# Attention with beacons and an MoE layer on one core: the first loads, a fourth buffer of probabilities, two of raw Q/K

## The chip, the cores and the metric

The kernel runs on one core of a Trainium2 chip. The metric is the device time of one execution in microseconds (us). Before the change the median of five runs is 351.29 us (350.4 to 353.74). Another execution was profiled; durations and waits come from that one.

## What is computed

For each of 8 batches and 8 heads there are 576 queries, keys and values of 64 elements, and 16 "beacon" keys and values in front of them. Every query sees all beacons, and the keys up to its own place. The heads' results are set side by side to a row of 512 elements per token (4608 tokens), and two matrix products follow with a leaky ReLU between them.

```python
scores = scale * np.matmul(q, k_all.transpose(0, 1, 3, 2))   # k_all: 16 beacons, then k
scores = np.where(causal, -1000000000.0, scores)
a = np.exp(scores - scores.max(-1, keepdims=True))
a /= a.sum(-1, keepdims=True) + 1e-09
attn = np.matmul(a, v_all)
x = attn.transpose(0, 2, 1, 3).reshape(B * S, H * D)
h = x @ w_in                    # 512 -> 2048
out = np.maximum(0.01 * h, h) @ w_out   # 2048 -> 512
```

## The kernel before, in words

**Head pairs.** The unit of attention is a pair of heads: 4 pairs to a batch, 32 in all, counted by `g`; `divmod(g, 4)` gives the batch and the place in it. Keys lie on the 128 partitions in five chunks (`ROWS`, `OFF`; the first has the 16 beacons and 112 keys). For a pair, `score(g, n)` (L295) makes four groups of transposed scores, n = 0 to 3, in PSUM: 2 x 512, 2 x 464, 2 x 416 and 2 x 288 columns, with causal parts that would be all zero left out. ScalarE takes each group's exponential out of PSUM (L315) into the pair's buffer of probabilities, `aT`. There are two PSUM buffers for scores (`ps_sc`), three of `aT` (`a_bufs`, L97) and three of the transposed keys `kT` (L98). The triangle on the diagonal is then set to zero: by VectorE with a stored triangle for pairs 0 and 1 (`masks_by_tri`, L335), by GpSimd with four affine selects for all others (`masks`, L346).

**Values.** `value(g, half)` (L368) multiplies the probabilities with `v_aug`, the values with a column of ones, in two halves of the queries: the first half needs chunks 0 to 2 of the values, the second all five. VectorE divides by the sums (L395, L396) into `x_nat`. `finish(g)` transposes `x_nat` on TensorE and VectorE copies it to `xT` (L413), from which the MoE part reads. Four PSUM buffers (`ps_one`) serve values, transposes and MoE groups alike.

**MoE.** Tokens go in 9 chunks of 512. `moe1` (L416) makes one group of 128 hidden units for a chunk: four matmuls and a leaky ReLU by ScalarE (L429); a chunk has 16 of them. `moe2` (L434) does a quarter of 128 tokens' output, also four matmuls. `fill()` (L464) issues the next group of either kind that is allowed. A chunk of tokens can start when the pairs that it needs are finished; the first one needs pair 3. Groups 0 to 7 of a chunk read the first half of `w_in`, groups 8 to 15 the second.

**Loads.** Queries and keys are loaded by GpSimd's queue, which casts float32 to bfloat16 on the way (`load_qk`, L120 and L133): a call for one batch and two pairs (`grp`), with `es` telling which of the two pairs. Tiles `q_raw` and `k_raw` come from `qkpool`, three buffers of each. Values are loaded in float32 on SyncE's queue (`load_v`, L209 to L218) in six DMAs, the first of which waits for the DMA that `after` names; `cast_v` casts them chunk by chunk, on GpSimd. Weights are loaded and cast by GpSimd's queue in halves (L110, L114). For batches 0 and 1, TensorE transposes queries and keys (`t_q`, L235, 18 small transposes each) and VectorE copies them out; from batch 2 on, GpSimd brings them into order (`permute`, L160), a transposing DMA on SyncE's queue turns them (`turn_pairs`, L266), and GpSimd copies them to their place (`in_order`, L279).

**The very first pair.** `load_first_pair` (L141) loads the queries of pair 0 in float32 on SyncE's queue and its keys in float32 on ScalarE's queue, behind the beacon keys of batches 0 and 1. VectorE casts the queries (L510), ScalarE and VectorE a half of the keys each (L511, L512). Ahead of them, `keep_busy(n)` (L477) lets TensorE do n products of the identity with itself, whose result nobody reads.

**Order.** The order on every engine is the order in which the program issues instructions (`manual_schedule`, L488)[...]. The last part of the program is therefore the schedule: a prologue, then a loop over `g` in which pairs 0 to 7 have orders written out by hand, and pairs from 8 on share one order in which MoE groups fill slots between scores and values. `loads(g)` and `loads_after(g)` put loads, casts and the DMA transposes into GpSimd's and SyncE's order.

Of the kernel before, what the change touches and what calls it, by code (L numbers as in the profile page):

```python
# [9 lines left out]
BF16 = mybir.dt.bfloat16  # L10
# [5 lines left out]
def kernel(  # L16
# [11 lines left out]
    nc = tc.nc  # L28

    B, H, S, D = q.shape  # L30
# [10 lines left out]
    RI = 9  # L41
    RP = S // RI
# [25 lines left out]

    singles = ctx.enter_context(tc.tile_pool(name="singles", bufs=1))
    rawpool = ctx.enter_context(tc.tile_pool(name="rawpool", bufs=2))  # L70
    qkpool = ctx.enter_context(tc.tile_pool(name="qkpool", bufs=3))
    natpool = ctx.enter_context(tc.tile_pool(name="natpool", bufs=2))
    turnpool = ctx.enter_context(tc.tile_pool(name="turnpool", bufs=2))
    headpool = ctx.enter_context(tc.tile_pool(name="headpool", bufs=2))
# [19 lines left out]
        for t in v_bufs:  # L94
            nc.gpsimd.memset(t[:, :, :, D : D + 1], 1.0)

    a_bufs = [singles.tile([128, 2, ACOLS], BF16, name=f"aT{i}") for i in range(3)]  # L97
    k_bufs = [singles.tile([128, NKB * 128], BF16, name=f"kT{i}") for i in range(3)]  # L98

    def make_pads():  # L100
# [16 lines left out]

    qk_raw = {}

    def load_qk(b, grp, es=(0, 1)):  # L120


        if (b, grp) not in qk_raw:
            qk_raw[b, grp] = (
                qkpool.tile([128, 2, RI, D], BF16, name="q_raw"),
                qkpool.tile([128, 2, RI, D], BF16, name="k_raw"),
            )
        for e in es:
            if b == 0 and grp == 0 and e == 0:
                continue  # L130
            h0 = 4 * grp + 2 * e
            for src, dst in zip((q, k), qk_raw[b, grp]):
                dma = nc.gpsimd.dma_start(  # L133
                    out=dst[e * RP : (e + 1) * RP],
                    in_=src[b, h0 : h0 + 2].rearrange("h (p i) d -> p h i d", i=RI),
                )
        return dma

    first_raw = []

    def load_first_pair():  # L141
        load_beacon_k(0, 2, nc.scalar)
        t = rawpool.tile([128, NKB, H, D], FP32, name="v_raw")
        flat = t[0:RP].rearrange("p c h d -> p (c h d)")
        n = 2 * RI * D
        for i in range(2):
            first_raw.append(flat[:, i * n : (i + 1) * n].rearrange("p (h i d) -> p h i d", h=2, i=RI))
        for eng, src, dst in zip((nc.sync, nc.scalar), (q, k), first_raw):
            last = eng.dma_start(out=dst, in_=src[0, 0:2].rearrange("h (p i) d -> p h i d", i=RI))
        return last  # L150


    first_cast = [
        natpool.tile([128, RI, 2, D], BF16, name=n)[0:RP].rearrange("p i e d -> p (i e d)").rearrange(
            "p (h i d) -> p h i d", h=2, i=RI
        )
        for n in ("q_nat", "k_nat")
    ]

    def permute(b, grp, which):  # L160

# [73 lines left out]
    def t_q(g, which, copy=nc.vector.tensor_copy):  # L235
# [10 lines left out]
            dst = kT[:, NB : NB + S]  # L246
        ps = ps_one.tile([128, 1024], BF16, name="tp", tag="one")
        raw = qk_raw[b, grp][which]
        if g == 0:
            raw = first_cast[which]  # L250
        for i in range(RI):
            for h in range(2):
                nc.tensor.transpose(
# [41 lines left out]
    def score(g, n):  # L295
        qT, kT = qk[g]
        if n == 0:
            probs[g] = a_bufs[g % 3]
        aT = probs[g]
        parts = SCORES[n]  # L300
        sc = ps_sc.tile([128, 2, 512], FP32, name="sc", tag="sc")
        c0 = parts[0][3]
        for c, q0, w, col in parts:
            for par in range(2):
                ps_ = slice(par * 64, par * 64 + 64)
                nc.tensor.matmul(  # L306
                    out=sc[:, par, col - c0 : col - c0 + w],
                    lhsT=kT[ps_, c * 128 : (c + 1) * 128],
                    rhs=qT[ps_, q0 : q0 + w],
                    start=True,  # L310
                    stop=True,
                    skip_group_check=True,
                )
        w = sum(p[2] for p in parts)
        nc.scalar.activation(  # L315
            out=aT[:, :, c0 : c0 + w], in_=sc[:, :, 0:w], func=AF.Exp, scale=0.125
        )
# [178 lines left out]
        }  # L496
    )
    with order:
        first = load_first_pair()
        make_identity(nc, ident)  # L500
        load_qk(0, 0)
        load_qk(0, 1)
        load_v(0, after=first)
        make_pads()
        cast_beacon_k(0, 2, nc.scalar.copy)
        keep_busy(24)
        beacon_transposes(0, 2)
        beacon_columns(0, nc.vector)
        beacon_columns(1, nc.vector)
        nc.vector.tensor_copy(out=first_cast[0], in_=first_raw[0])  # L510
        nc.scalar.copy(out=first_cast[1][:, 0], in_=first_raw[1][:, 0])  # L511
        nc.vector.tensor_copy(out=first_cast[1][:, 1], in_=first_raw[1][:, 1])  # L512
        keep_busy(18)
        t_q(0, 0)
        keep_busy(4)
        t_q(0, 1, nc.scalar.copy)
        keep_busy(3)
        make_tri()
        make_ones()
        beacon_columns(2, nc.gpsimd)  # L520
        cast_v(0, nc.gpsimd, 0, 1)
        load_qk(1, 0, (0,))

        def loads(g):
            b, hp = divmod(g, NPAIR)
            if g == 1:
                beacon_columns(3, nc.gpsimd)
                cast_v(0, nc.gpsimd, 1, 3)
                load_v(1, after=load_qk(1, 0, (1,)))
                cast_v(0, nc.gpsimd, 3, 5)  # L530
                load_w_in(0)
            elif g == 2:
                beacon_columns(4, nc.gpsimd)
            elif g == 3:
# [38 lines left out]
        for g in range(NG + 3):  # L573
            if has(g):
                loads(g)

            if g < 5:

                score(g, 0)
                score(g, 1)  # L580
                t_q(g + 1, 0)
                t_q(g + 1, 1)
                if g in (1, 2):
                    masks_by_tri(g - 1)
                if g >= 3:
                    value(g - 2, 0)
                if g < 2:
                    keep_busy(3)
                score(g, 2)
# [3 lines left out]
                if g < 2:  # L593
                    keep_busy(4)
                if g == 2:
                    value(g - 2, 0)
                if g >= 2:
                    value(g - 2, 1)
                if g >= 3:
                    finish(g - 3)  # L600
                if g > 1:
                    masks(g)
                if g == 4:
                    value(3, 0)
                continue

            if g == 5:

                score(5, 0)
                value(3, 1)  # L610
                score(5, 1)
                finish(2)
                score(5, 2)
                finish(3)
                fill()
                score(5, 3)
                masks(5)
                fill()
                t_q(6, 0)
                t_q(6, 1)  # L620
                fill()
                fill()
                continue

            if g == 6:
# [14 lines left out]
                load_beacon_k(2, B, nc.gpsimd)  # L640
                fill()
                fill()
                value(4, 0)
                value(4, 1)
                continue

            if g == 7:
                score(7, 0)
                score(7, 1)
                value(5, 0)  # L650
                finish(4)
                value(5, 1)
                score(7, 2)
                score(7, 3)
                load_qk(2, 0)
                masks(7)
                finish(5)
                value(6, 0)
                fill()
                value(6, 1)  # L660
                fill()
                fill()
                finish(6)
                value(7, 0)
                fill()
                value(7, 1)
                fill()
# [4 lines left out]
            if g == 8:  # L672
# [8 lines left out]
                while done1[0] + done2[0] < 22:  # L681
                    fill()
                beacon_transposes(2, B)
                while done1[0] + done2[0] < 30:
                    fill()
                in_order(8)
                in_order(9)
# [75 lines left out]
```

## Time and profile before

| | before |
|---|---|
| median of five runs | 351.29 us |
| the profiled execution | 351.35 us |
| its span, first to last instruction | 349.5 us |
| TensorE busy (share of the span) | 339.3 us (97%) |
| ScalarE busy | 187.4 us (54%) |
| GpSimd busy | 196.5 us (56%) |
| VectorE busy | 98.0 us (28%) |
| moved by DMA | 40.88 MB, 117 GB/s on average |

The profile names engines PE (TensorE; PEld is its weight load), DVE (VectorE), ACT (ScalarE), POOL (GpSimd) and SP (SyncE); a q behind a name is an engine's DMA-issuing side. In a timeline, a row has its start and its duration in us, then engine, line, operation and "result<-sources", and in brackets how long the engine had been idle before it and what released it; rows of one kind in a row are merged (x12). In the chain of waits, a row has a start and a duration in us, and then what the end of the program was waiting for at that time. In a table by stretches, a row has the stretch, its length, the busy time and number of instructions of each engine, the granted clock of TensorE, the mean busy share of the DMA engines, and the GB/s that they moved.

### The profile page before, as it was taken

How to read it: one execution, taken by the hardware profiler on the slowest of the kernel's cores; microseconds unless marked ns; L12 is line 12 of the kernel's file. 1: busy time of each engine (PE TensorE's matmuls, PEld its weight loads, DVE VectorE, ACT ScalarE, POOL GpSimd, SP SyncE). 2: the span in 40 equal slices, each digit the busy share in tenths (PEclk: the TensorE clock that was granted, in tenths of full speed). 3: DMA queues.
4: the chain of work that ended last, by engine and by line, in shares of the span. 5: the costliest groups of instructions: out<-in, count | busy, mean ns of one | idle time of the engine just before them, and what ended most of it. 6: DMA issues, size and time to landing. Idle time of an engine off the chain costs nothing.

```text
span 349.5 us, 7405 instructions
## 1 busy us (share of the span) xinstructions
PE 339.3 (97%) x3045; PEld 171.7 (49%) x3045; DVE 98.0 (28%) x240; ACT 187.4 (54%) x277; POOL 196.5 (56%) x335
## 2 busy tenths in 40 slices
PE   7889999899999999999999999999999999999996
PEld 6565554334554444444544444455444554444444
DVE  3794530123342222322321223222321331000121
ACT  4978756565456863486347833784368304633300
POOL 7596926688899799777976779667321100000000
PEclk9999999999999999999999999999999999999999
DMA  8999999968988894992489419980110011000012
GB/s 164 198 159 200 181 213 158 191 120 160 227 167 122 158 164 96 187 197 54 79 181 184 93 33 192 183 125 31 49 45 0 2 73 49 0 30 32 30 60 92
DMA packets 85121, 40.88 MB, mean 117 GB/s; under 512 B 69040, under 2 KB 79280, under 8 KB 85088
## 3 DMA queue, kind: packets, MB, share of 16 engines
q1 hardware_dynamic: 72544, 26.52, 36.4%
q0 software_dynamic: 12128, 13.54, 25.1%
q10 hardware_dynamic: 416, 0.36, 0.5%
q8 instruction: 24, 0.39, 0.5%
q14 instruction: 9, 0.07, 0.1%
HBM read 37.22 MB, written 9.44 MB: 134 GB/s over the span
## 4 chain that ended last, share of the span: by engine, by line
PE 79%; DMA 12%; POOL 3%; DVE 2%; SPq 2%; issue 1%; ACT 0%; POOLq 0%
PE acc L444 36%; PE acc L422 28%; PE av L386 7%; PE sc L306 6%; DMA v_raw<-in_v_dram 5%; DMA bk_raw<-in_beacon_k_dram 4%; DMA q_turn<-q_nat 1%; PE tp L408 1%; DMA v_raw<-in_k_dram 1%; DVE osb L453 1%; SPq L218 1%; POOL v_aug L227 1%; DVE xT L413 1%; POOL w_out_sb L114 0%; POOL aT L355 0%
## 5 line engine op out<-in xcount | busy, mean ns | idle before, releaser
L422 PE MATMUL acc<-xT,w_in_sb 128*128 128x512 bf16 x576 | 139.3, 379 | 1.6 <-DVE xT L413 1.4
L315 ACT ACTIVATE aT<-sc 128x1024 bf16<-128x1024 f32 (+3 forms) x128 | 103.7, 869 | 66.7 <-PE sc L306 66.7
L444 PE MATMUL acc<-w_out_sb,gT 128*128 128x512 bf16 (+1 forms) x592 | 139.0, 374 | 0.0
L429 ACT ACTIVATE gT<-acc 128x512 bf16<-128x512 f32 x144 | 85.8, 601 | 74.2 <-PE acc L422 73.9
L444 PEld LDWEIGHTS <-gT 128*128 128x128 bf16 x592 | 53.2, 98 | 58.4 <-issue 6.1
L422 PEld LDWEIGHTS <-w_in_sb 128*128 128x128 bf16 x576 | 51.8, 98 | 59.6 <-issue 4.6
L453 DVE COPY osb<-acc 128x512 f32<-128x512 f32 (+1 forms) x37 | 25.1, 677 | 128.8 <-PE acc L444 128.0
L355 POOL TENSOR_SCALAR_AFFINE_SELECT aT<-aT 128x224 bf16<-128x224 bf16 (+1 forms) x120 | 48.7, 450 | 18.6 <-PE av L386 9.9
L286 POOL COPY qT<-q_turn 128x576 bf16<-128x576 bf16 x24 | 28.6, 1191 | 40.2 <-PE sc L306 21.2
L386 PEld LDWEIGHTS <-aT 128*128 128x128 bf16 (+1 forms) x960 | 36.9, 98 | 15.5 <-issue 2.4
L386 PE MATMUL av<-v_aug,aT 128*128 128x65 bf16 (+1 forms) x960 | 40.0, 194 | 0.7 <-POOL v_aug L227 0.7
L306 PE MATMUL sc<-qT,kT 64*128 64x80 bf16 (+4 forms) x384 | 35.8, 283 | 3.0 <-ACT aT L315 1.5
L396 DVE TENSOR_TENSOR x_nat<-av,rec 128x384 bf16<-128x384 f32 x64 | 31.4, 491 | 2.2
L286 POOL COPY kT<-k_turn 128x576 bf16<-128x576 bf16 x24 | 28.6, 1190 | 0.8 <-DMA k_turn<-k_nat 0.6
L413 DVE COPY xT<-tp 128x576 bf16<-128x576 bf16 x32 | 14.5, 453 | 45.2 <-PE tp L408 45.2
L395 DVE RECIPROCAL rec<-av 128x6 f32<-128x6 f32 x64 | 11.9, 186 | 52.8 <-PE av L386 52.8
L306 PEld LDWEIGHTS <-kT 64*128 64x128 bf16 x384 | 12.3, 94 | 28.5 <-issue 16.2
L227 POOL CAST v_aug<-v_raw 128x512 bf16<-128x512 f32 (+1 forms) x35 | 20.6, 632 | 5.9 <-DMA v_raw<-in_v_dram 5.9
L133 POOL DMA_DIRECT2D q_raw<-in_q_dram x31 | 19.6, 632 | 5.1 <-DMA w_out_sb<-in_moe_w_out_dram 4.9
L133 POOL DMA_DIRECT2D k_raw<-in_k_dram x31 | 19.7, 634 | 3.8 <-DMA w_out_sb<-in_moe_w_out_dram 2.8
L408 PEld LDWEIGHTS <-x_nat 128*128 128x128 bf16 (+2 forms) x160 | 11.1, 97 | 6.7 <-DVE rec L395 0.2
L167 POOL COPY q_nat<-q_raw 128x1152 bf16<-128x1152 bf16 x12 | 13.9, 1160 | 0.4 <-DMA q_raw<-in_q_dram 0.4
(43 smaller groups left out, 92.3 us busy)
## 6 DMA issues: line engine op xcount, KB each, us to landing
out_dram<-osb SPq DMA_DIRECT2D x35, 256.0 KB, 2.4
v_raw<-in_v_dram SPq DMA_DIRECT2D x24, 256.0 KB, 5.1
q_raw<-in_q_dram POOLq DMA_DIRECT2D x31, 144.0 KB, 5.6
k_raw<-in_k_dram POOLq DMA_DIRECT2D x31, 144.0 KB, 5.8
w_in_sb<-in_moe_w_in_dram POOLq DMA_DIRECT2D x2, 1024.0 KB, 9.4
w_out_sb<-in_moe_w_out_dram POOLq DMA_DIRECT2D x2, 1024.0 KB, 13.2
v_raw<-in_v_dram SPq DMA_DIRECT2D x8, 224.0 KB, 4.0
v_raw<-in_v_dram SPq DMA_DIRECT2D x8, 160.0 KB, 4.5
```

What stands on the lines that cost most here:

```text
L133: dma = nc.gpsimd.dma_start(out=dst[e * RP : (e + 1) * RP], in_=src[b, h0 : h0 + 2].rearrange("h (p i) d -> p h i d", i=RI),)
L227: eng.tensor_copy(out=dst[0 : ROWS[c], c, :, 0:D], in_=t[0 : ROWS[c], c])
L286: nc.gpsimd.tensor_copy(out=dst.rearrange("c (p i) -> c p i", i=RI), in_=t[:, :, e].rearrange("c i p -> c p i"),)
L306: nc.tensor.matmul(out=sc[:, par, col - c0 : col - c0 + w], lhsT=kT[ps_, c * 128 : (c + 1) * 128], rhs=qT[ps_, q0 : q0 + w], start=True, s ...
L315: nc.scalar.activation(out=aT[:, :, c0 : c0 + w], in_=sc[:, :, 0:w], func=AF.Exp, scale=0.125)
L355: nc.gpsimd.affine_select(out=part, in_=part, compare_op=ALU.is_ge, fill=0.0, base=base, channel_multiplier=-1, pattern=pattern,)
L386: nc.tensor.matmul(out=avv[:, n, 0 : D + 1], lhsT=aT[0 : ROWS[c], par, a0 : a0 + 128], rhs=va[0 : ROWS[c], c, 2 * hp + par, :], start=(c = ...
L396: nc.vector.tensor_tensor(out=x_nat[:, t0:t1].rearrange("p t e d -> p (t e) d"), in0=avv[:, :, 0:D], in1=rec[:, n0:n1, None].to_broadcast( ...
L422: nc.tensor.matmul(out=acc, lhsT=w_in_sb[:, j, fc * 128 : (fc + 1) * 128], rhs=xT[:, j, i * 512 : (i + 1) * 512], start=(j == 0), stop=(j ...
L429: nc.scalar.activation(out=gT[i][:, fc, :], in_=acc, func=AF.Prelu, alpha=0.01)
L444: nc.tensor.matmul(out=acc[:, 0:w], lhsT=gT[i][:, fc, t * 128 : (t + 1) * 128], rhs=w_out_sb[:, fc, c0 : c0 + w], start=(fc == 0), stop=(f ...
L453: nc.vector.tensor_copy(out=osb[:, 0:w], in_=acc[:, 0:w])
```

## The change

Five things change.

1. `load_first_pair`: queries of pair 0 are loaded by GpSimd's casting queue, straight to bfloat16, as the first instruction of that queue, ahead of the making of the identity. Keys of pair 0 are loaded in float32 on SyncE's queue. ScalarE's queue has the beacon keys alone. The cast of the queries on VectorE falls away; the keys' cast stays split between ScalarE and VectorE.
2. `a_bufs` goes from three to four buffers, `qkpool` from three to two.
3. The prologue has fewer fillers (10, 14, 1 and 3 instead of 24, 18, 4 and 3), the values of batch 0 wait for the second pair's keys instead of the first pair's, and the cast of chunk 0 of the values moves behind the start of pair 1. Both pairs of batch 1's first group are loaded at once, right behind that cast, and the first half of `w_in` is requested two chunk casts earlier.
4. The orders of pairs 2 to 7 are written anew: values of pair 0 come behind the scores of pair 2 and inside pair 3; values of pair 4 move from pair 6 to behind the scores of pair 7; two MoE groups move from pair 5 to pair 7.
5. Before pair 8, 31 MoE groups are issued instead of 30.

The core of the diff:

```diff
-    qkpool = ctx.enter_context(tc.tile_pool(name="qkpool", bufs=3))
+    qkpool = ctx.enter_context(tc.tile_pool(name="qkpool", bufs=2))
-    a_bufs = [singles.tile([128, 2, ACOLS], BF16, name=f"aT{i}") for i in range(3)]
+    a_bufs = [singles.tile([128, 2, ACOLS], BF16, name=f"aT{i}") for i in range(4)]
...
+    def qk_rows(b, grp, e):
+        h0 = 4 * grp + 2 * e
+        return [src[b, h0 : h0 + 2].rearrange("h (p i) d -> p h i d", i=RI) for src in (q, k)]
...
         load_beacon_k(0, 2, nc.scalar)
...
-        for eng, src, dst in zip((nc.sync, nc.scalar), (q, k), first_raw):
-            last = eng.dma_start(out=dst, in_=src[0, 0:2].rearrange("h (p i) d -> p h i d", i=RI))
+        load_qk(0, 0, ())
+        q_rows, k_rows = qk_rows(0, 0, 0)
+        nc.sync.dma_start(out=first_k[0], in_=k_rows)
+        nc.gpsimd.dma_start(out=qk_raw[0, 0][0][0:RP], in_=q_rows)
...
-            probs[g] = a_bufs[g % 3]
+            probs[g] = a_bufs[g % 4]
...
-        first = load_first_pair()
+        load_first_pair()
         make_identity(nc, ident)
-        load_qk(0, 0)
+        load_v(0, after=load_qk(0, 0, (1,)))
         load_qk(0, 1)
-        load_v(0, after=first)
         make_pads()
         cast_beacon_k(0, 2, nc.scalar.copy)
-        keep_busy(24)
+        keep_busy(10)
         beacon_transposes(0, 2)
+        nc.scalar.copy(out=first_cast[:, 0], in_=first_k[0][:, 0])
+        nc.vector.tensor_copy(out=first_cast[:, 1], in_=first_k[0][:, 1])
         beacon_columns(0, nc.vector)
-        beacon_columns(1, nc.vector)
-        nc.vector.tensor_copy(out=first_cast[0], in_=first_raw[0])
-        nc.scalar.copy(out=first_cast[1][:, 0], in_=first_raw[1][:, 0])
-        nc.vector.tensor_copy(out=first_cast[1][:, 1], in_=first_raw[1][:, 1])
-        keep_busy(18)
+        keep_busy(14)
         t_q(0, 0)
-        keep_busy(4)
+        keep_busy(1)
         t_q(0, 1, nc.scalar.copy)
         keep_busy(3)
+        beacon_columns(1, nc.vector)
         make_tri()
         make_ones()
         beacon_columns(2, nc.gpsimd)
-        cast_v(0, nc.gpsimd, 0, 1)
-        load_qk(1, 0, (0,))
...
             if g == 1:
+                cast_v(0, nc.gpsimd, 0, 1)
+                load_v(1, after=load_qk(1, 0))
                 beacon_columns(3, nc.gpsimd)
                 cast_v(0, nc.gpsimd, 1, 3)
-                load_v(1, after=load_qk(1, 0, (1,)))
+                load_w_in(0)
                 cast_v(0, nc.gpsimd, 3, 5)
-                load_w_in(0)
...
-            if g < 5:
+            if g < 3:
...
                 if g == 2:
-                    value(g - 2, 0)
-                if g >= 2:
-                    value(g - 2, 1)
...
+                    value(0, 0)
+                    masks(2)
                 continue
+            if g == 3:
+                score(3, 0)
+                score(3, 1)
+                t_q(4, 0)
+                t_q(4, 1)
+                score(3, 2)
+                value(0, 1)
+                score(3, 3)
+                masks(3)
+                value(1, 0)
+                value(1, 1)
+                finish(0)
+                continue
+            if g == 4:
+                score(4, 0)
+                score(4, 1)
+                t_q(5, 0)
+                t_q(5, 1)
+                value(2, 0)
+                score(4, 2)
+                value(2, 1)
+                finish(1)
+                score(4, 3)
+                masks(4)
+                continue
             if g == 5:
                 score(5, 0)
+                value(3, 0)
+                score(5, 1)
                 value(3, 1)
-                score(5, 1)
                 finish(2)
                 score(5, 2)
                 finish(3)
-                fill()
                 score(5, 3)
                 masks(5)
                 fill()
                 t_q(6, 0)
                 t_q(6, 1)
-                fill()
                 fill()
...
-                value(4, 0)
-                value(4, 1)
                 continue
             if g == 7:
                 score(7, 0)
                 score(7, 1)
+                fill()
+                fill()
+                score(7, 2)
+                score(7, 3)
+                masks(7)
+                load_qk(2, 0)
+                value(4, 0)
+                value(4, 1)
                 value(5, 0)
                 finish(4)
                 value(5, 1)
-                score(7, 2)
-                score(7, 3)
-                load_qk(2, 0)
-                masks(7)
+                value(6, 0)
                 finish(5)
-                value(6, 0)
-                fill()
                 value(6, 1)
                 fill()
-                fill()
+                value(7, 0)
                 finish(6)
-                value(7, 0)
                 fill()
                 value(7, 1)
...
-                while done1[0] + done2[0] < 30:
+                while done1[0] + done2[0] < 31:
                     fill()
```

## The prediction

> **What bounds it now.** First the page: engine totals, the DMA slices and the shares of the chain of waits.
>
> ```profile
> PE 339.3 (97%) x3045; PEld 171.7 (49%) x3045; DVE 98.0 (28%) x240; ACT 187.4 (54%) x277; POOL 196.5 (56%) x335
> ...
> DMA  8999999968988894992489419980110011000012
> ...
> PE 79%; DMA 12%; POOL 3%; DVE 2%; SPq 2%; issue 1%; ACT 0%; POOLq 0%
> ```
>
> TensorE (PE) is full, so only its gaps, its fillers and late starts can be won; the DMA engines are full for the first 60 us (seven slices of 8.7 us). From 65.4 us on the chain is TensorE alone, and the change leaves that order of groups as it was. So the case is decided before 65.4 us. Second, the timeline of the first 30 us:
>
> ```profile
> 8.12 9.40 ACT L315 ACTIVATE aT<-sc 128x1024 bf16<-128x1024 f32 x12 [0.19 <-PE sc L306]
> ...
> 17.49 0.61 POOL L227 CAST v_aug<-v_raw 80x512 bf16<-80x512 f32 x1 [0.48 <-DMA v_raw<-in_v_dram]
> ...
> 18.16 0.35 PE L386 MATMUL av<-v_aug,aT 80*128 80x65 bf16 x6 [0.66 <-POOL v_aug L227]
> ...
> 18.44 0.59 PE L306 MATMUL sc<-qT,kT 64*128 64x512 bf16 x4
> ...
> 18.87 3.16 ACT L315 ACTIVATE aT<-sc 128x1024 bf16<-128x1024 f32 x4 [1.35 <-PE sc L306]
> ```
>
> Exponentials run without a gap from 8.12 us for pairs 0 to 2. Then pair 3 waits 1.35 us, because the second half of pair 0's values stands ahead of its scores on TensorE and needs the fifth chunk of V. The first MoE group starts at 28.00 us and lasts 1.02, 0.16 over the usual 0.86. Third, the chain in order of time, which shows the only long TensorE stall after that:
>
> ```profile
> 40.05 15.07 DMA bk_raw<-in_beacon_k_dram
> ...
> 57.94 5.07 DMA q_turn<-q_nat
> ...
> 63.06 1.17 POOL qT L286
> 64.23 1.10 POOL kT L286
> 65.33 0.05 issue
> 65.37 0.59 PE sc L306 x4
> ```
>
> Scores of pair 8 start at 65.37 us after 1.07 us of idleness, late because of a chain of loads (V of batch 1, the weights, the beacons, Q/K of batch 2). So two clocks set the end: when TensorE gets there (64.3) and when the data are there (65.37). A gain on one alone becomes a wait on the other. Fourth, the table by stretches (DMA share and GB/s last) shows where loads have room:
>
> ```profile
> 9.10:13.50 4.40, 4.12 (x80) 2.64 (x77) 2.40 (x5) 4.40 (x7) 1.86 (x4) 1.00 1.27 237
> 13.50:19.60 6.10, 4.84 (x126) 3.27 (x122) 5.56 (x14) 4.75 (x7) 5.35 (x11) 1.00 0.91 137
> 19.60:30.00 10.40, 9.78 (x194) 6.57 (x186) 8.17 (x21) 9.15 (x13) 7.33 (x19) 1.00 1.12 187
> ```
>
> 137 GB/s against about 190 for 6.1 us is about 1.7 us of unused loading, just where the change issues batch 1's Q/K and the first weights earlier.
>
> **The start.** Removed: one ScalarE-queue load (K) and VectorE's cast of Q, 0.76 us. Moved: K to SyncE's queue at 0.81 us, Q to GpSimd's queue at about 0.81, ahead of the identity; on that queue everything behind it (identity, six loads) slips by one issue, 0.72 us. The issue answers bound the landing of Q:
>
> ```profile
> v_raw<-in_q_dram SPq DMA_DIRECT2D x1, 288.0 KB, 3.9
> ```
> ```profile
> q_raw<-in_q_dram POOLq DMA_DIRECT2D x1, 144.0 KB, 5.1
> ```
> ```profile
> q_raw<-in_q_dram POOLq DMA_DIRECT2D x1, 144.0 KB, 3.0
> ```
>
> SyncE's at 0.81 us took 3.9; GpSimd's at 1.52, behind Q, K and beacons on the engines, 5.1; GpSimd's at 75.01, alone, 3.0. [...] By the rows it lands between 3.8 (alone) and 5.9 (contended). At 0.81 us nothing else is moving, so I take a value nearer the first: 4.6. K takes Q's place on SyncE and should land at about 4.7, not 5.97. Before, landing of K to first exponential took 8.12 - 5.97 = 2.15, so 6.85 at best.
>
> TensorE can hold that back. The identity comes 0.72 us later, and the fillers ahead of Q's transposes fall from 42 to 24. Before, the first 24 fillers took 2.74 us (114 ns each), the next 18 1.27 (71): the clock came up between. [...] With TensorE's start at 2.15 instead of 1.43, [...] by the row alone, 0.72 later, 5.1. Two sets of 18 transposes at half clock cost about 0.4 us each more (0.47 in the row). First exponential: 7.2 to 8.3, I take 7.7, a gain of 0.4.
>
> **Pairs 0 to 5.** With a fourth probabilities buffer, values of pair 0 come after the scores of pair 2 and 3, so the 1.35 us wait need not recur. What is late next is GpSimd: between the casts of chunk 0 and chunk 1 it now issues four loads of batch 1. Chunk 0's cast began at 11.64; I take 11.6, as the V loads now wait for another load that lands near 6.3 against 5.97, while less data is ahead of them. Cast 0.6, four issues 2.4, beacon columns 0.2, two casts 1.3: 16.1. TensorE is ready for the first half of values at 7.7 + 8.4 (16.50 - 8.12 before) = 16.1. So scores of pair 3 start at 16.1 + 0.1 + 0.47 = 16.7 (18.44 before). Start-to-start durations of the timeline: two wide scores 0.51, transposes of Q and K 0.69, value halves 0.47 and 0.57, narrow scores 0.28 and 0.23, transposes of x 0.26; exponentials 0.92, 0.84, 0.75, 0.63. Pair 3: scores and transposes to 17.9, exponential until 18.1, third score to 18.4, second half of pair 0's values to 19.0 (chunk 4 landed at 17.44, cast 0.6, with the weight issue of 0.78 now ahead: about 18.5), fourth score to 19.3, values of pair 1 and x of pair 0 to 20.6. Pair 4 then starts at 20.6 (21.93 before) and pair 5 at 23.75, when a score buffer comes free (25.80 before). Values of pair 3 need GpSimd's masks at 24.0; its queue (casts, two loads, masks of 1.6 each) has them at 23.7, a thin 0.3. Pair 5's scores and x of pair 3 end at 26.8, where the first group starts. The first weights, issued at about 16.2 instead of 18.05 and 9.4 us under way, are there at 25.6: hidden, with 1.2 to spare; if that cover fails, their lateness counts in full. Before, 28.00 plus 0.16 plus one narrow score of 0.23; so TensorE is 1.6 us ahead.
>
> **Pairs 6, 7 to 65 us.** The groups ahead of pair 8's scores go from 30 to 31, 0.86 us of work moved, not added. From 26.8: 31 x 0.864 = 26.8, scores 2.04, transposes 1.38, values of pairs 4 to 7 4.16, x 1.04, beacons 0.3: 35.7. Bubbles: the same sum for before gives 63.1 against 64.3, so 1.2, of which 0.5 was the wait for the second weights (gone: they are asked for later) and 0.16 the x copy. New: values of pairs 4 to 6 stand together, and VectorE needs 1.8 us a pair (0.74 + 0.59 + 0.45) where TensorE needs 1.3: 0.5 to 1.0 more. I take 1.4. TensorE arrives at 63.9.
>
> Data: the weights are issued 1.9 us earlier, V of batch 1 waits behind them and comes as much earlier, and so its casts, the second weights and the rest: 65.37 - 1.9 = 63.5. Bounds: 0 to 2.7. The later of the two is 63.9: 1.47 earlier and one group further: **2.3 us**. Fewer fillers are in this sum already. The Q/K buffers from three to two cost nothing: the transposes that free them end by about 15 us for loads issued at 12.3 and 21; without that cover GpSimd's queue stops for as long. Two more pad memsets lie at 1 to 1.5 us on an idle VectorE, and pair 1's beacon columns move there behind a copy that pair 0 needs first. After pair 8, key copies had 1.2 us or more to spare.
>
> **Rivals.** *The data chain does not move*: the DMA engines are full anyway and the order of bytes is nearly the same; pair 8 starts at 65.37 still, only a group further: 0.87 us, 350.4. For it: shares over 1.0 from 19.6 us on. Against: the 137 GB/s stretch lies ahead of it. *V starves, slower*: four Q/K loads and the weights are on GpSimd's queue beside V's last chunks. V of batch 1, beside such loads, took up to 12.0 us (issued 20.68, landed 32.66). If chunks 3 and 4 of batch 0, issued at 10.0 and 11.0, do the same, they land at 23, the second half of pair 0's values starts at 23.6, not 18.4, and 5.2 - 2.3 = 2.9 us are lost: 354.2. It decides from a cast of chunk 4 that ends after about 20.7. Against: before, these chunks shared the engines with two such loads and landed at 15.36 and 17.44.
>
> **The numbers.** The profiled execution took 351.35 us, its span 349.5, the median is 351.29. The forecast is 351.35 - 2.3, rounded 349.1: chance 0.62, own range 347.8 to 350.0 (a start at 7.2, no VectorE bubbles and data at 62.7 give 348.0; a late start and 0.7 us of GpSimd's lateness 349.8). The first rival 0.18, the second 0.20. Measurement tells about 0.5% (1.76 us) from no change; of the forecast 0.55 lies beyond it, so faster 0.55, same 0.25, slower 0.20. Range 347.8 to 352.0.
>
> **What would show it.** First exponential at about 7.7; no wait of ScalarE over 1 us between pairs 2 and 3; scores of pair 3 at 16.7, the first group at 26.8, pair 8 at 63.9 with little or no wait for GpSimd's key copy; the first weights landed before 26. A wait of over 1 us there means the first rival; TensorE waiting for the cast of V after 20 us the second.

## The result and the profile after

| | before | after |
|---|---|---|
| median, timed side by side on one chip | 351.59 us (49 executions, 350.4 to 353.74) | 353.67 us (28 executions, 351.38 to 355.2) |
| ratio, with 95% interval | | 1.0049 [1.0036, 1.0062] |
| the profiled execution | 351.35 us | 354.79 us |
| its span | 349.5 us | 353.1 us |
| first MoE group starts | 28.00 us | 32.51 us |
| scores of pair 8 start | 65.37 us | 69.69 us |

The ratio is that of the measurement, with its interval, and not the quotient of the two medians. Three executions that took over 1.5% longer than the fastest of their kernel (one of e3_fewer, two of the kernel before) are left out of the ratios and of the counts without a fall-back below. The change makes the kernel slower by about 0.5%. The forecast was 349.1 us with a range of 347.8 to 352.0, so it had the wrong sign and the measured time lies outside the range. The profiled execution, 354.79 us, is one of the slower ones of its kernel. First the page of the kernel after, the same three lines as before:

```profile
PE 344.9 (98%) x3024; PEld 174.3 (49%) x3024; DVE 99.0 (28%) x241; ACT 187.9 (53%) x277; POOL 196.4 (56%) x336
...
DMA  8999899969997793995299509870110011000012
...
PE 95%; DVE 3%; issue 1%; POOL 0%; ACT 0%; POOLq 0%
```

TensorE has 21 instructions fewer and is busy for 5.6 us more. That is the line to stumble over: fewer matmuls cannot take longer unless some of them do. DMA has left the chain of waits (12% before), TensorE has taken its place. TensorE's timeline shows where it grew:

```profile
2.69 1.25 PE L481 MATMUL av<-ident 128*128 128x128 bf16 x10 [2.69 <-POOL ident masks.py:199]
...
3.95 1.70 PE L481 MATMUL av<-ident 128*128 128x128 bf16 x14
5.58 0.69 PE L252 MATMUL tp<-ident,q_raw 64*64 64x64 bf16 x18
...
7.60 0.99 PE L305 MATMUL sc<-qT,kT 64*128 64x512 bf16 x4
8.53 0.69 PE L252 MATMUL tp<-ident,q_raw 64*64 64x64 bf16 x18
...
12.28 0.99 PE L305 MATMUL sc<-qT,kT 64*128 64x512 bf16 x4
...
16.95 0.99 PE L305 MATMUL sc<-qT,kT 64*128 64x512 bf16 x4
```

The same places in the timeline of the kernel before:

```profile
5.88 0.47 PE L253 MATMUL tp<-ident,q_nat 64*64 64x64 bf16 x18 [0.43 <-DVE q_nat L510]
...
7.68 0.58 PE L306 MATMUL sc<-qT,kT 64*128 64x512 bf16 x4 [0.22 <-ACT kT L259]
...
10.78 0.39 PE L306 MATMUL sc<-qT,kT 64*128 64x512 bf16 x2
```

A row of 18 transposes takes 0.69 us after and 0.47 before, four wide scores 0.99 and 0.58. In the kernel after there is hardly any idle time between the rows (0.08 us of the 22.98 from 2.69 to 25.67), and yet pairs 0, 1 and 2 follow each other at 4.67 us instead of 3.1: TensorE is at half clock (e10_31_fill, below, has 0.99 for the same four scores in a stretch whose granted clock is on record as 0.50), and it bounds what ScalarE bounded before. This lasts until the rows shrink between 24 and 27 us, in the same timeline further on:

```profile
24.23 0.42 PE L305 MATMUL sc<-qT,kT 64*128 64x208 bf16 x4
...
26.34 0.59 PE L305 MATMUL sc<-qT,kT 64*128 64x512 bf16 x4
26.86 0.47 PE L252 MATMUL tp<-ident,q_raw 64*64 64x64 bf16 x18
...
32.51 1.04 PE L421 MATMUL acc<-xT,w_in_sb 128*128 128x512 bf16 x4
```

The trace's own clock records begin when the clock first becomes full: at 25.67 us after, at 4.38 us before. The granted-clock column of the stretches cannot show this, because it prints 1.00 for any time ahead of the first record. The stretch from 12 to 17 us, first of the kernel after and then of an experiment (e4_orders, below) that had its clock at 6.81 us; the columns are those of the tables by stretches above:

```profile
12.00:17.00 5.00, 5.00 (x68) 2.91 (x66) 3.07 (x5) 3.70 (x5) 4.82 (x9) 1.00 1.00 186
```

```profile
12.00:17.00 5.00, 4.40 (x109) 2.88 (x108) 4.31 (x7) 5.00 (x7) 4.58 (x9) 1.00 1.13 182
```

Both say 1.00. But 68 matmuls fill 5.00 us in one and 109 fill 4.40 in the other, and ScalarE, always busy in the second, is at 3.70 in the first. Count and busy time tell the clock here, the column does not.

The sum closes. The first group is 4.51 us later. From there to pair 8's scores it takes 37.18 us for 31 groups; before it took 37.37 for 30, of which 1.07 was the wait for the keys. Pair 8 is 4.32 us later with one group of 0.86 more behind it: 3.46 us. The profiled executions differ by 3.44.

### The profile page after: what moved, and what is told of

Read it like the earlier page. It is cut to its first block, busy times and chain, and to the rows that moved or that the text cites. A ratio compares the mean times of both kernels' runs of the same rounds, so it can differ in the third digit from the quotient of the medians.

```text
span 353.1 us, 7366 instructions
## 1 busy us (share of the span) xinstructions
PE 344.9 (98%) x3024; PEld 174.3 (49%) x3024; DVE 99.0 (28%) x241; ACT 187.9 (53%) x277; POOL 196.4 (56%) x336
## 4 chain that ended last, share of the span: by engine, by line
PE 95%; DVE 3%; issue 1%; POOL 0%; ACT 0%; POOLq 0%
PE acc L443 36%; PE acc L421 35%; PE sc L305 10%; PE av L385 9%; PE tp L252 2%; PE tp L407 2%; PE av L481 2%; DVE osb L452 1%; DVE xT L412 1%; DVE x_nat L395 1%; DVE qT L258 0%; DVE kT L258 0%; PE tp L187 0%; DVE rec L394 0%; ACT kT L258 0%
## 5 line engine op out<-in xcount | busy, mean ns | idle before, releaser
L285 POOL COPY qT<-q_turn 128x576 bf16<-128x576 bf16 x24 | 28.6, 1193 | 41.6 <-PE sc L305 24.9
L305 PE MATMUL sc<-qT,kT 64*128 64x80 bf16 (+4 forms) x384 | 38.0, 301 | 0.4 <-DVE kT L258 0.4
L407 PE MATMUL tp<-ident,x_nat 128*128 128x128 bf16 (+2 forms) x160 | 14.0, 214 | 0.5 <-DVE x_nat L395 0.5
```

Source lines behind the costliest of these rows:

```text
L285: nc.gpsimd.tensor_copy(out=dst.rearrange("c (p i) -> c p i", i=RI), in_=t[:, :, e].rearrange("c i p -> c p i"),)
L305: nc.tensor.matmul(out=sc[:, par, col - c0 : col - c0 + w], lhsT=kT[ps_, c * 128 : (c + 1) * 128], rhs=qT[ps_, q0 : q0 + w], start=True, s ...
L407: nc.tensor.transpose(ps[:, q0 : q0 + rows], x_nat[0:rows, t].rearrange("p e d -> p (e d)"), ident[0:rows, 0:rows],)
```

## The experiments

My theory after the result: the late clock, made by the later identity and the fewer fillers, is the loss (*clock*). Against it stood: the new orders cost by themselves (*orders*), or the changed loads do (*loads*). All experiments are timed in five rounds beside the kernel before. The table has times of each one's profiled execution (clock: when it is first full, and for how long it later fell back to half), then all executions. "No fall-back": how many executions had a mean granted clock over 0.998 by their own record (in the profiled executions one fall-back of 3.4 us gave 0.995, of 6.8 us 0.99), and their median. That mean does not see a late first full clock, as there is no record ahead of it (after has 1.000).

| | clock first full, us | half again, us | first group, us | pair 8, us | median, us (n) | ratio to before | no fall-back: of how many, median |
|---|---|---|---|---|---|---|---|
| before | 4.38 | | 28.00 | 65.37 | 351.6 to 352.0 | 1 | 121 of 193, 351.14 |
| after | 25.67 | | 32.51 | 69.69 | 353.67 (28) | 1.0049 [1.0036, 1.0062] | 19 of 29, 353.66 |
| e1_fillers | 6.59 | 3.4 | 30.30 | 67.49 | 352.31 (22) | 1.0026 [1.0004, 1.0048] | 16 of 22, 351.99 |
| e2_identity | 17.43 | | 30.92 | 68.11 | 352.66 (16) | 1.0031 [1.0009, 1.0053] | 13 of 16, 352.70 |
| e3_fewer | 19.68 | | 33.15 | 68.96 | 352.7 (22) | 1.0019 [0.9997, 1.0042] | 19 of 21, 352.47 |
| e4_orders | 6.81 | | 29.25 | 66.44 | 351.54 (22) | 1.0007 [0.9985, 1.0029] | 17 of 22, 351.39 |
| e5_both | 6.22 | 3.4 | 29.91 | 67.10 | 352.36 (14) | 1.0011 [0.9985, 1.0036] | 4 of 14, 351.23 |
| e6_none | 14.13 | | 29.24 | 65.24 | 353.38 (22) | 1.005 [1.003, 1.007] | 22 of 22, 353.38 |
| e7_nomask | 5.53 | | 27.81 | 65.38 | 351.48 (14) | 1.0014 [0.999, 1.0038] | 9 of 14, 351.16 |
| e8_late | 6.59 | | 29.16 | 66.35 | 351.93 (22) | 1.002 [0.9999, 1.004] | 13 of 22, 351.28 |
| e9_31 | 6.94 | | 28.69 | 65.39 | 351.05 (22) | 0.9988 [0.9969, 1.0006] | 15 of 22, 350.77 |
| e10_31_fill | 4.89 | 6.8 | 30.82 | 67.27 | 352.1 (14) | 0.9993 [0.9971, 1.0016] | 6 of 14, 350.90 |
| e11_first | 7.05 | | 30.37 | 68.35 | 352.51 (22) | 1.001 [0.9991, 1.0029] | 7 of 22, 351.69 |
| e12_orders_fill | 5.61 | 3.4 | 29.87 | 66.84 | 351.65 (22) | 1.0 [0.9982, 1.0018] | 16 of 22, 351.28 |

**e1_fillers**: after, with the fillers of before.

```diff
-        keep_busy(10)
+        keep_busy(24)
...
-        keep_busy(14)
+        keep_busy(18)
...
-        keep_busy(1)
+        keep_busy(4)
```

> The changed kernel with the fillers of before again (24, 18 and 4 instead of 10, 14 and 1); all else stays changed. In the changed kernel's profile TensorE's full clock is granted only at 25.7 us (4.4 us before), and pairs 0 to 2 follow each other at 4.7 us instead of 3.1. Theory C (the late clock, from fewer and later fillers, is the whole loss): the clock comes within the first 9 us, a pair takes 3.1 to 3.2 us, the first group starts at 27 to 28 us, and the median falls by about 3 us to 350.7 or less. Theory O (the new orders of pairs 2 to 7 and their values on VectorE cost the time, whatever the clock): the median stays within 1 us of 353.7.

The clock was full at 6.59 us. It fell back once (20.24 to 23.66 us), and the fillers held the first scores up until 8.79. The ratio went from 1.0049 to 1.0026 and its interval still excludes 1, so the fillers alone do not undo all of the loss. By these values they undo about half, but the two intervals overlap. The median lies between what the two theories expected.

**e2_identity**: after, with the identity ahead of the first load of Q.

```diff
-        load_first_pair()
         make_identity(nc, ident)
+        load_first_pair()
```

> The changed kernel with the identity made ahead of the first query load on GpSimd's queue, fillers as changed (10, 14, 1). TensorE should start at about 1.4 us again instead of 2.69. Theory C in the form 'it started too late': the clock comes within 9 us and the median falls to about 351. Theory C in the form 'the fillers are too few or too thin': full clock still comes late (over 15 us) in the profile, and the median stays at 353 to 354. Theory O: 353.7 with either clock.

TensorE began at 1.43 us as before, and Q was there in time: first scores at 7.22, the earliest of all. The clock still came only at 17.43, with 24 fillers ahead of Q's transposes and an idle gap of 0.65 us between them. The ratio went to 1.0031.

**e3_fewer**: before, with the fillers of after and nothing else.

```diff
-        keep_busy(24)
+        keep_busy(10)
...
-        keep_busy(18)
+        keep_busy(14)
...
-        keep_busy(4)
+        keep_busy(1)
```

> The kernel before with the fewer fillers of the change (10, 14 and 1 instead of 24, 18 and 4), nothing else changed; the identity still comes first. Theory C: the full clock comes late in many executions and the median rises by 1.5 to 3.5 us, to 353 to 355. Theory O: within 0.7 us of before, 351.6.

The same picture appears in a kernel with the old loads and orders. Its stretch from 12 to 17 us, to be laid beside the two above:

```profile
12.00:17.00 5.00, 5.00 (x66) 2.94 (x64) 2.09 (x4) 3.70 (x5) 4.59 (x9) 1.00 1.09 178
```

66 matmuls in 5.00 us: half clock, full at 19.68. Pair 8 starts 3.59 us later than before, and the whole execution takes 3.48 us longer (354.83 us): in this profile the late clock, from the fillers alone, is paid in full. In the median less is lost than expected, and the interval of the ratio just includes 1. The executions without a fall-back reach from 350.65 to 354.83 us (those of the kernel before end at 352.5), so not every one seems to pay it.

**e4_orders**: before, with the buffers, the 31 groups and the orders of pairs 2 to 7 of after; its prologue and loads are those of before.

```diff
-    qkpool = ctx.enter_context(tc.tile_pool(name="qkpool", bufs=3))
+    qkpool = ctx.enter_context(tc.tile_pool(name="qkpool", bufs=2))
-    a_bufs = [singles.tile([128, 2, ACOLS], BF16, name=f"aT{i}") for i in range(3)]
+    a_bufs = [singles.tile([128, 2, ACOLS], BF16, name=f"aT{i}") for i in range(4)]
...
-                while done1[0] + done2[0] < 30:
+                while done1[0] + done2[0] < 31:
```

> The kernel before with the new orders of pairs 2 to 7, the fourth buffer of probabilities, two raw Q/K buffers and 31 groups, but with the prologue, the first pair's loads, the fillers and the loads of pair 1 as before. Theory C: the clock comes at about 4.4 us as before and the orders bring their gain, so the median is 0.5 to 2 us below 351.6. Theory O: 353 or more, with the clock early.

No loss against the kernel before and no gain: *orders* falls as the reason for the loss. Why nothing is gained is seen in its timeline:

```profile
17.05 3.19 DVE L343 TENSOR_TENSOR aT<-aT,tri 128x224 bf16<-128x224 bf16 x3
...
20.39 0.56 DVE L396 TENSOR_TENSOR x_nat<-av,rec 128x384 bf16<-128x384 f32 x1
...
21.00 1.38 PE L386 MATMUL av<-v_aug,aT 128*128 128x65 bf16 x30 [0.72 <-DVE x_nat L396]
```

The stall of before ahead of pair 3 is gone (17.49 us instead of 18.44), but the values of pair 1 then stand ahead of pair 4's scores. VectorE masks pair 1 from 17.05 to 20.24, one piece of it taking 2.42 us where the others take 0.38 to 0.66, and only then does pair 0's division, for which TensorE waits 0.72 us. Pair 4 starts at 23.08 (before: 21.93), and the first group at 29.25, not earlier than before. A part of this is the clock, full at 6.81 instead of 4.38: e9_31, which has the orders of before and its clock at 6.94, has 22.41 and 28.69.

**e5_both**: after, with both cures of the start at once.

```diff
-        load_first_pair()
         make_identity(nc, ident)
+        load_first_pair()
...
-        keep_busy(10)
+        keep_busy(24)
...
-        keep_busy(14)
+        keep_busy(18)
...
-        keep_busy(1)
+        keep_busy(4)
```

> The changed kernel with the identity first and with the fillers of before (24, 18, 4): both of TensorE's start conditions as before, while the loads, the buffers and the orders stay changed. Theory C (the clock's late start is the whole loss): the clock comes early as often as in the kernel before, and the median is like that of the orders alone, 351.0 to 351.9. Theory L (the changed loads of the first pair and of pair 1 cost time too): 352.3 or more, with an early clock in the profile.

First group 29.91, 2.6 us earlier than after; the ratio's interval includes 1. Against e4_orders it differs only in the loads and the casts that go with them. What TensorE waited for from 8 to 30 us, and the stretch from 20 us on:

```profile
PE tp L252 <- DMA q_raw<-in_q_dram: 0.6, 1, 0.6
...
PE av L385 <- POOL v_aug L225: 0.4, 2, 0.2
```

```profile
20.00:23.50 3.50, 3.50 (x59) 2.86 (x58) 2.48 (x6) 1.77 (x3) 3.50 (x10) 0.53 1.03 156
```

Pair 4's queries and the casts of V now come late, both between 17 and 19.2 us, and at 19.87 the clock falls to half (here the column does show it: 0.53). 10 of its 14 executions had a fall-back, against 5 of 22 of e4_orders; the four without took 351.23 in the median, so what this kernel still loses goes with the fall-backs. That the loads bring them is not shown: e1_fillers, with the same loads, had 6 of 22, and e10_31_fill, with the loads of before, 8 of 14.

**e6_none**: before, without the fillers of the prologue.

```diff
-        keep_busy(24)
...
-        keep_busy(18)
...
-        keep_busy(4)
...
-        keep_busy(3)
```

> The kernel before without any filler in the prologue (0 instead of 24, 18, 4 and 3; those inside pairs 0 and 1 stay). Theory C: nothing warms TensorE before the scores, full clock comes later than 15 us in nearly every execution, and the median rises by 2 to 3.5 us to 353.6 to 355. If the fillers do not set the clock: no change, or some tenths less, since they stand ahead of nothing.

353.38 us, ratio 1.005 [1.003, 1.007]: as large a loss as that of the changed kernel, from the fillers alone, though by a stronger cut (none left of 49, where the change leaves 28). None of its 22 executions had a recorded fall-back. That the late first full clock makes the loss in each of them is argued, as only the profiled one has its time of full clock on record (14.13 us, a little before the 15 expected). And this one, with 352.56 us one of the better ones, did not lose directly by it: TensorE reached pair 8 at 65.24 us, no later than before, because the late start went into the 1.07 us wait there. It lost its time ahead of pair 12:

```profile
93.24 0.58 PE L306 MATMUL sc<-qT,kT 64*128 64x512 bf16 x4 [1.39 <-POOL kT L286]
```

The kernel before has no such wait there. Why the key copy came late is not known.

**e7_nomask**: e4_orders without VectorE's triangle of pair 1.

```diff
-                if g > 0:
-                    masks_by_tri(g - 1)
+                if g == 1:
+                    masks_by_tri(0)
```

> The orders-alone kernel with pair 1's triangle mask on VectorE left out, so the output of pair 1 is not masked. In the orders-alone profile values of pair 1 wait 0.7 us on TensorE for VectorE, which is busy with that mask (one piece of it 2.4 us long beside GpSimd) and scores of pair 4 start at 23.08. Theory V (VectorE bounds pairs 2 to 4 in the new orders): scores of pair 4 start at 21.0 to 22.0, the first group at 27.5 to 28.5, and the median falls by 0.5 to 1.5 us. If VectorE is not the bound there: 23 and 29.2 us, and the same median.

```profile
20.10 1.10 PE L386 MATMUL av<-v_aug,aT 128*128 128x65 bf16 x30
...
21.39 0.59 PE L306 MATMUL sc<-qT,kT 64*128 64x512 bf16 x4
...
27.81 0.39 PE L422 MATMUL acc<-xT,w_in_sb 128*128 128x512 bf16 x1
```

With that VectorE work away, the values follow without a gap, pair 4 starts at 21.39 instead of 23.08 and the first group at 27.81 instead of 29.25: VectorE held these pairs. (The piece of 2.42 us in e4_orders is the longest of its kind in all profiles, 0.22 to 1.63 in the others, so 1.44 us may be more than these orders lose as a rule.) But of this 1.44 us only 1.06 reach pair 8 (65.38 instead of 66.44), and the median without a fall-back is 351.16 against 351.39. The chain of waits says why:

```profile
58.34 4.48 DMA q_turn<-q_nat
...
62.94 1.18 POOL qT L286
...
64.15 1.17 POOL kT L286
65.32 0.14 POOL kT L284
```

Pair 8's keys are ready at 65.3 us, as before, and now TensorE waits for them: the rest of what was won on one side goes into the wait on the other, and anything more would too.

**e8_late**: before, with the buffers and the new orders of pairs 6 and 7 and 31 groups, but the old orders of pairs 2 to 5 (without two groups in pair 5).

```diff
                 score(7, 1)
-                value(5, 0)
-                finish(4)
-                value(5, 1)
+                fill()
+                fill()
                 score(7, 2)
                 score(7, 3)
-                load_qk(2, 0)
                 masks(7)
-                finish(5)
+                load_qk(2, 0)
+                value(4, 0)
+                value(4, 1)
...
-                while done1[0] + done2[0] < 30:
+                while done1[0] + done2[0] < 31:
```

> The kernel before with a fourth buffer, two raw Q/K buffers, the new orders of pairs 6 and 7 and 31 groups, but with the old orders of pairs 2 to 5 (except for the two groups that left pair 5) and the old prologue. Theory V (the new orders of pairs 2 to 5 give away what those of 6 and 7 bring): at an early clock scores of pair 4 start at 21.9 and the first group at about 28.2, scores of pair 8 between 65.2 and 65.6, and the median is 0.5 to 1.0 us under before, at 350.6 to 351.1. If the orders of 6 and 7 give away more than they bring: 351.6 or more.

First group at 29.16 (expected 28.2), with the new orders of pairs 2 to 5 (e4_orders) 29.25: these bring nothing. The median, too, is above the one expected.

**e9_31**: before, with 31 groups ahead of pair 8 and nothing else.

```diff
-                while done1[0] + done2[0] < 30:
+                while done1[0] + done2[0] < 31:
```

> The kernel before with 31 groups instead of 30 ahead of pair 8's scores, nothing else. In its profile TensorE waits 1.07 us there for the key copy at 65.37, which came no earlier in any variant (65.2 to 67.0). Theory D (the data chain is fixed, and only the place of a group can be won): scores of pair 8 start at 65.2 to 65.6 with a wait of 0.1 to 0.3 us, a gain of 0.7 to 0.9 us at an early clock, and a median 0.3 to 0.9 us under before. If the group only moves the wait: no change.

```profile
64.58 0.86 PE acc L444 x4
65.45 0.53 PE sc L306 x4
```

In its chain of waits, TensorE's 31st group now ends where pair 8's keys are ready (65.33): the 1.07 us wait of before has been filled with work. 351.05 us against 351.98 beside it, the best median of all; the ratio's interval [0.9969, 1.0006] still includes no change. With the same 31 groups and the clock up at nearly the same time, e4_orders and e8_late reach pair 8 at 66.44 and 66.35 us, this kernel at 65.39: in the profiles the new orders cost about 1 us, which the 31st group covers. The medians without a fall-back point the same way (351.39 and 351.28 against 350.77), but the ratios cannot be told apart.

**e10_31_fill** (e9_31 with 30 fillers instead of 18) and **e12_orders_fill** (e4_orders with the same) try whether longer dense work secures the clock.

```diff
-        keep_busy(18)
+        keep_busy(30)
```

> As e9_31, and 30 fillers instead of 18 behind the beacons' transposes, so that dense work lasts to about 6 us (clock up) or 7.4 us (not). Theory C: full clock comes early in more executions, so the share of times above 352 falls from about 4 in 10 to under 2 in 10 and the median is 350.3 to 350.9, the best of all. If the fillers only cost their time: 351.5 or more.

> The orders-alone kernel with 30 fillers instead of 18. Theory C: an early clock in more executions, but TensorE here arrives after the data, so a longer start is not absorbed: median 351.2 to 351.8, above e10_31_fill by 0.5 to 1 us. If the new orders are the better ones at an early clock: 350.5 or less.

It does not, in either: 6 of 14 executions of e10_31_fill and 16 of 22 of e12_orders_fill had no fall-back. Only the median expected of e12_orders_fill came true (351.65), but not that it would lie above that of e10_31_fill. In the profiled executions the clock came at 4.89 and 5.61 us, but fell back in the middle of the attention, at 18.55 us for 6.8 us in the first and at 19.26 for 3.4 in the second. The rows of e10_31_fill ahead of its fall-back:

```profile
17.92 0.44 PE L386 MATMUL av<-v_aug,aT 128*128 128x65 bf16 x9 [0.47 <-POOL v_aug L227]
18.81 0.49 PE L386 MATMUL av<-v_aug,aT 80*128 80x65 bf16 x6 [0.46 <-POOL v_aug L227]
19.23 0.99 PE L306 MATMUL sc<-qT,kT 64*128 64x512 bf16 x4
```

TensorE waits twice for half a microsecond, and from then on works at half clock (0.99 for four scores).

**e11_first**: e5_both, with the values' casts and batch 1's loads in the order of before, so that of the loads only the first pair's are changed, and with them the load that batch 0's values wait for.

```diff
+        cast_v(0, nc.gpsimd, 0, 1)
+        load_qk(1, 0, (0,))
...
-                cast_v(0, nc.gpsimd, 0, 1)
-                load_v(1, after=load_qk(1, 0))
...
-                load_w_in(0)
+                load_v(1, after=load_qk(1, 0, (1,)))
                 cast_v(0, nc.gpsimd, 3, 5)
+                load_w_in(0)
```

> As e5_both (identity first, fillers as before, all else changed), but with the loads and casts of pair 1 in the order of before: two of batch 1's Q/K loads behind the first V cast, two later, and the first weights behind all casts. It differs from the orders-alone kernel by the first pair's loads alone. Theory L1 (pair 1's loads are the cost: four loads hold GpSimd ahead of the casts, TensorE waits 0.2 to 0.6 us for casts and Q, and its clock falls back at 19.9 us): no half clock after the start, scores of pair 4 at 23.0 to 23.3, first group at 29.2 to 29.5, median about 351.5. Theory L2 (the first pair's loads are the cost): first group near 29.9 and 352.3 as e5_both.

```profile
PE acc L421 <- DMA w_in_sb<-in_moe_w_in_dram: 1.7, 1, 1.7
PE tp L252 <- DMA k_raw<-in_k_dram: 0.9, 2, 0.7
```

The waits for loads remain with the first pair's loads alone, the first weights come late as well (landed at 30.09 us), and 15 of 22 executions had a fall-back. So putting batch 1's loads back is no cure; which of the two load changes weighs more is not separated.

## Why the prediction was wrong, point by point

**The start: this is the step that failed.** Its landing times were right in size: Q by GpSimd's queue landed at 5.30 us (taken: 4.6, with 5.9 as the late end), K by SyncE's at 4.84 (4.7), each 4.0 us after its issue began; the first exponential began at 8.26 (7.7, an estimate; before 8.12). The step that failed is the full clock, "by the row alone, 0.72 later, 5.1". It was 25.67 us. Two terms were wrong. The identity was one issue later by 0.72 us in the sum; GpSimd's first issue began only at 1.32, and the identity was ready 1.26 us later than before:

```profile
1.32 0.73 POOL L149 DMA_DIRECT2D q_raw<-in_q_dram  x1 [0.81 <-POOLq L760]
...
2.35 0.29 POOL masks.py:199 TENSOR_SCALAR_AFFINE_SELECT ident<-ident 128x128 bf16<-128x128 bf16 x1
```

And fewer fillers were booked as a saving ("in this sum already"), but the early clock was lost with them: by cutting them alone it is full at 19.68 us in e3_fewer and at 14.13 in e6_none instead of 4.38, and with only the identity mended (e2_identity) it stays late, 17.43. I priced half clock for two sets of transposes only, at 0.4 us each (measured 0.69 instead of 0.47, so 0.22), and not for the scores behind them. I took the place of the row at which the clock came up as something that shifts with TensorE's start; I did not price the case in which it does not come for a long time. How many fillers there are does not order the times among the late ones: none gave 14.13 us, 28 gave 17.43, 19.68 and 25.67, and all 49 from 4.38 to 7.05 (one profile each). In the changed kernel TensorE was busy for 22.90 of the 22.98 us from 2.69 to 25.67 and, by its rows, at half clock all that time, so a TensorE that the trace shows busy is no guarantee of full clock. What it takes beyond that stays open. Price, in the profiled executions: from first scores to first group 24.9 us, in e4_orders, with the same orders and the clock up, 21.1, so 3.8 us.

**Pairs 0 to 5.** The wait ahead of pair 3 did go away as predicted (ScalarE's idle time there is 0.34 us, not 1.35), but under the half clock, and scores of pair 3 came at 20.64 instead of 16.7. Even with the clock up, 26.8 for the first group was wrong: e4_orders has 29.25, e8_late with the old orders 29.16. The sum counted TensorE and GpSimd; the new orders put pair 1's values behind VectorE, whose mask and division were costed at nothing there. e7_nomask shows it by taking the mask away (27.81). The 1.0 us that is left to 26.8 is not taken apart.

**Pairs 6 and 7** were right as a number: 31 groups to pair 8 took 37.18 us, predicted were 37.1 with bubbles of 1.4. But the new orders are no gain there: from pair 5's first scores to pair 8's, e9_31 with the old ones and the same 31 groups takes 39.12 us, e8_late with the new ones 39.85. The bubbles are VectorE's, as expected. In the chain of the kernel after:

```profile
44.53 0.56 DVE x_nat L395
...
45.21 0.42 DVE x_nat L395
...
45.77 0.56 DVE x_nat L395
46.33 0.37 DVE xT L412
...
46.82 0.43 DVE x_nat L395
```

**The data, 1.9 us earlier, failed too.** The weights were issued at 16.45 instead of 18.05, but landed at 27.03 instead of 27.44; pair 8's keys were ready at 66.32, in no experiment earlier than 64.87, and in none with the changed loads earlier than 65.92. The unused 1.7 us of loading did not carry over. So the first rival's mechanism is true for the data, and even with a full clock hardly more than the moved group, 0.87 us, was to be had; e9_31 has it in its profile for one changed number.

**The second rival did not occur**: chunk 4 of the values was cast at 18.93 us, ahead of the 20.7 from which it was to decide. The loss came from a case that was no rival of mine: the clock.

**The changed loads** are the rest. With the start mended (e5_both), 10 of 14 executions had a fall-back; TensorE's waits for late Q, K and V stand ahead of it in the profile. That these waits cause it is argued, not shown. In the four profiled executions with a fall-back, TensorE was idle for 0.90 to 1.15 us of the 3.4 us ahead of it; but the kernel before was idle for 1.01 us between 14.62 and 18.03 us and e11_first for 1.66 between 27.53 and 30.94, and neither fell back. And the three other kernels with these loads (after, e1_fillers, e2_identity) had fall-backs in 10 of 29, 6 of 22 and 3 of 16 executions only. What decides it stays open, and with it the price of the changed loads, whose ratios (e5_both 1.0011, e4_orders 1.0007) cannot be told apart.

## What to carry to other kernels

The early clock can hang on work that nobody reads (one profile each: full between 4.38 and 7.05 us with all 49 fillers, between 14.13 and 25.67 with 28 or none): before such work is cut or moved, ask what happens if the clock does not come up, and price the whole stretch at half clock, here 3.8 us in the profiled execution, about 2 us between the medians, for 21 fillers fewer and an identity 1.26 us later. Read the clock from the duration of equal rows (here 0.99 and 0.58 us for four wide scores), since a busy TensorE and a clock column of 1.00 do not show it. And where two chains meet within about 1 us of each other (here 64.3 and 65.4), a gain on one is worth no more than the gap: fill the gap with work that is already there, as the one moved group does.

## What the runs showed of the hardware beyond that

The spread of one kernel's times goes largely with the clock. Of the kernel before's 193 executions beside the experiments, 121 had no fall-back after the first full clock and a median of 351.14 us; 14 with a mean granted clock of about 0.995 had 352.21, 46 with 0.99 352.57, 11 with 0.985 353.98, one with 0.981 354.6. The fall-backs in the profiled executions lasted 3.41, 3.41, 3.41 and 6.83 us: three times one length and once twice that. A small VectorE multiplication (80 partitions, two times 80 columns) took 2.42 us in e4_orders while GpSimd cast values and issued the weights' load, and 0.22 to 1.63 in the other profiles; what makes the difference was not tested. And a 1024 KB load by GpSimd's queue that was issued 1.6 us earlier landed 0.4 us earlier: it took 10.58 us instead of 9.4, so that the earlier place in a busy queue was worth a quarter of itself here.
